# Attention and an ELU network on one core: an order planned in rounds by deadlines, the later pairs' first 64 queries in float16 with DMA transposes, and one copy for the first batches' outputs

## The chip, the core and the metric

The kernel runs on 1 core of a Trainium2 chip. The core's engines run on their own and wait for each other by semaphores: TensorE (PE in the profile; PEld is its loading of stationary operands), VectorE (DVE), ScalarE (ACT), GpSimd (POOL) and SyncE (SP), whose queue issues every DMA of this kernel, one after the other. Times are device microseconds (us) of one execution; lower is better.

## The reference

```python
scores = scale * np.matmul(q, k.transpose(0, 1, 3, 2))        # 8 batches, 8 heads, 576 x 64 each
bias = -(cum[:, :, :, None] - cum[:, :, None, :])             # cum: cumulative sum of max(s, 0)
scores = np.where(causal, -1000000000.0, scores + np.minimum(bias, 0.0))
attn = np.exp(scores - np.max(scores, axis=-1, keepdims=True))
attn = attn / (np.sum(attn, axis=-1, keepdims=True) + 1e-09)
attn_out = np.matmul(attn, v)
x = attn_out.transpose(0, 2, 1, 3).reshape(4608, 512)
h = x @ w_in                                                  # 512 -> 2048
g = np.where(h > 0.0, h, np.exp(np.minimum(h, 0.0)) - 1.0)
out = g @ w_out                                               # 2048 -> 512
```

The two weights come as 64-bit floats, the rest as 32-bit floats.

## The kernel before

**Work.** Attention goes by pairs of heads. A batch's 576 queries are its first 64, of both heads of a pair in one tile of 128 rows (a pair unit, tiles named `_None`), and four blocks of 128 queries per head. The first 320 queries of batches 0 to 2 (12 pairs, the low pairs; tiles `kl`, `sml`, `trl`, `tl`, `avl`, `xl`) are computed in float32. All else, the first 320 queries of batch 3, batches 4 to 7 whole, and the last 256 queries of batches 0 to 3, uses scores and values split in two float16 parts. So 20 pair units (batches 3 to 7) go the later way. For each block PE makes scores (`sc`), DVE adds the mask and finds the row's extreme (`mn`), ACT takes exp, the row is scaled by its inverse sum (`sm`, `sml`), turned, and multiplied by the values (`av`, `avl`); the result goes by `x` or `xl` to `x_dram`.

In a pair unit of before, the probabilities `psh` stay in float32; PE turns them (`tr`, line 1227), ACT or DVE copies the turned tile to `pc` and DVE subtracts to get its rest (`split_pt`, L1157 to L1162), PE multiplies twice (`av_None`, L1220), and `halves` (L1282) takes the wanted quarter-tiles out with two copies and two additions, both of 64x64. A block of 128 queries instead is split in float16 (`halved`) and turned by a DMA (`turned_load`, tile `T`). A low pair's result is put in `xl` by three copies (L890 to L894).

The network runs over 18 chunks of 256 rows. Chunk 0 is in float32 (`h<-x,wa`, `o<-wa,gg`); the others take each product as three float16 products (L1436, L1493), from weights split in two parts (`wp`). Each of the 32 weight units of 512 KB is loaded as raw 64-bit words into one of 4 slots (`raws`), decoded by ACT and DVE (L702, L706, L711), measured (L632, L635), and, when all are there, scaled and split (L437 to L439, L726).

**Order.** Nothing runs in the order of the code. Each operation is recorded with a priority, the engines it may run on and a cost for each (`Plan.op`), and `issue` lays them out: of all operations whose inputs are laid out, it takes the one that could start first by its own costs, of equal ones the one of lower priority number, and fixes the engine and the place. PE's order, for one, is then fixed: a matmul whose input is late holds all behind it. While PE's planned time is under 60 us, gaps are filled with transposes of the identity that nobody reads (`scratch`, L1556).

Of the kernel before, what the change touches and what calls it, by code (L numbers as in the profile page):

```python
# [10 lines left out]
F32R = mybir.dt.float32r  # L11
# [47 lines left out]
class Buf:  # L59


    def __init__(self, pool, shape, dtype, name, tag=None, bufs=1, others=(), always=False):
# [8 lines left out]
        self.users = 0  # L71
        self.until = {}
# [20 lines left out]
class Op:  # L93
    __slots__ = ("ways", "after", "before", "behind", "bufs", "new", "prio", "ready", "left", "filler")


class Plan:
# [45 lines left out]
    def op(self, prio, ways, reads=(), writes=(), late=()):  # L143
# [5 lines left out]
        for accesses, write in ((reads, False), (writes, True)):  # L149
# [10 lines left out]
            for b, part in expanded:  # L160
# [5 lines left out]
                if b not in o.bufs:  # L166
                    o.bufs.add(b)
                    b.users += 1
# [19 lines left out]
        o.left, o.ready = len(o.after) + len(firsts), {}  # L188
# [10 lines left out]

    def issue(self):  # L200
        engines = sorted({self.ENGINE.get(w[0], w[0]) for o in self.ops for w in o.ways})
# [3 lines left out]
        slots, skipped = {}, {}  # L205
        pipe = 0.0
# [13 lines left out]
        while pending:  # L220
# [7 lines left out]
            best = None  # L228
# [5 lines left out]
            for o in pending:  # L234
# [16 lines left out]
                else:  # L251
# [9 lines left out]
                    rank = (start + GAP if o.filler else start, o.prio)  # L261
                    if best is None or rank < best[0]:
                        best = (rank, o, n)
            assert best is not None, "no operation can be issued"
            (start, _), o, n = best
# [8 lines left out]
            if len(o.ways[n]) > 3:  # L274

                pipe = max(pipe, end) + o.ways[n][4] / RATE
                lag = pipe + o.ways[n][3] - end
            self.log.append((engine, start, end, o.prio))
            free[engine] = max(start + 40.0, end - self.OVERLAP.get(engine, 0.0))
            for b, k in o.new:  # L280
                gone = skipped.setdefault(b.home, set())
                gone.add(k)
                while taken[b.home] in gone:
                    gone.remove(taken[b.home])
                    taken[b.home] += 1
                slots.setdefault(b.key, []).append(b)
# [8 lines left out]
            for d in (*o.before, *o.behind):  # L295
                d.left -= 1
                if not d.left:
                    pending.append(d)
            at = len(block.instructions)
# [11 lines left out]
        return max(free.values()), free  # L311
# [53 lines left out]
def kernel(  # L365
# [55 lines left out]
    def rounded(prio, n, dst, src, reads, writes, sign=1.0, only=None):  # L421

        ways = [
            ("Pool", pool_1(n),
             lambda: pool.tensor_scalar(dst(), src(), sign, 1.0, ALU.mult, ALU.mult)),
            ("ACT", act_s(n),
             lambda: act.activation(dst(), src(), AF.Copy, scale=sign)),
            ("DVE-SB", dve_1(n),
             lambda: dve.tensor_scalar(dst(), src(), sign, None, ALU.mult)),
        ]  # L430
        op(prio, [w for w in ways if only is None or w[0] in only], reads, writes)

# [9 lines left out]
    def rest(prio, n, dst, src, hi, reads, writes, only=None):  # L442

        ways = [
            ("DVE-SB", dve_2(n), lambda: dve.tensor_tensor(dst(), src(), hi(), ALU.subtract)),
            ("Pool", pool_2(n), lambda: pool.tensor_tensor(dst(), src(), hi(), ALU.subtract)),
        ]
        op(prio, [w for w in ways if only is None or w[0] in only], reads, writes)
# [166 lines left out]

    def scale_tiles():
# [29 lines left out]
    def scales_of(prio, spans, dst):  # L646
# [20 lines left out]
        op(prio, [("PE", pe4(P), lambda: pe_.matmul(flat.v[:, :P], tops.v, ident, start=True, stop=True))],  # L667
# [174 lines left out]
    def weighing_low(u):  # L842
# [6 lines left out]
        def pair():  # L849
# [3 lines left out]
            op(prio, [("PE", pe4(P), lambda: pe_.matmul(  # L853
                av.v[:HB, n : n + P], u.vs.v[:, 0], turned.v[:, :P], start=True, stop=True))],
               [(turned, "pair"), u.vs], [av])

        def keys(kb):
# [22 lines left out]
            def products():  # L880
                for h in range(2):
                    pe_.matmul(av.v[h * HB : (h + 1) * HB, n - c : n], u.vs.v[:, 1 + 2 * kb + h], dst()[:, h],
# [147 lines left out]
    def prepare(u):  # L1030
# [14 lines left out]
        u.vs = plan.buf(sb, [P, 1, 2, D], F32R, f"vs_{u.tag}", tag="vs0", bufs=NP)  # L1045
        if u.col == 4:
            prio = PRIO_V
        src, used = (lambda: u.va.v[:, j, :1]), values_of(u.va, j)
        rounded(prio, D, lambda: u.vs.v[:, :1, 0], src, used, [u.vs])
        rest(prio, D, lambda: u.vs.v[:, :1, 1], src,  # L1050
             lambda: u.vs.v[:, :1, 0].bitcast(F32), used, [u.vs])
# [105 lines left out]
    def split_pt(prio, tag, tr, w):  # L1157
        pc = plan.buf(sb, [P, 2, w], F32R, f"pc_{tag}", tag="pc")
        psum_copy(prio, w, lambda: pc.v[:, 0], lambda: tr.v[:, :w], [tr], [(pc, 0)])
        op(prio, [("DVE", dve_p(w), lambda: dve.tensor_tensor(  # L1160
            pc.v[:, 1], tr.v[:, :w], pc.v[:, 0].bitcast(F32), ALU.subtract))],
           [tr, (pc, 0)], [(pc, 1)])  # L1162
        return [(pc, 0), (pc, 1)]

    def scoring(u):
# [8 lines left out]
        if u.h is None:  # L1174
            sm = plan.buf(sb, [P, 1], F32, f"sm_{u.tag}", tag="sm", bufs=2)
            psh = u.pp = plan.buf(sb, [P, P], F32, f"psh_{u.tag}", tag="pc")

            def pair():
# [6 lines left out]
                    (sm, 0, True, 1, 1.0), view=lambda v: v.rearrange("p (h t) -> p h t", h=2),  # L1185
# [476 lines left out]
```

## Time and profile before

| | |
|---|---|
| median of 3 runs | 1032.26 us (1030.23 to 1032.54) |
| the profiled execution | 1028.56 us, of which the span of its instructions is 1026.4 us |
| PE busy | 1005.4 us (98%) |
| PEld, DVE, ACT, POOL busy | 67%, 83%, 64%, 24% |

Busy time is the time in which an engine shows at least one instruction. Matmuls overlap each other in their rows, so a wait of PE shows only where it is longer than what is still running.

### The profile page before, as it was taken

The page shows a single profiled execution, that of the slowest core. Times are in us where ns is not written, and L with a number is a line of the kernel's source. Part 1 is how long each engine was busy: PE and PEld are TensorE (multiplying, and loading weights), DVE is VectorE, ACT ScalarE, POOL GpSimd, SP SyncE. Part 2 cuts the span into 40 slices and gives each one's busy share as a digit, 9 for nine tenths or more (in the row PEclk, how much of TensorE's full clock was granted, in tenths as well). Part 3 has the DMA queues.
Part 4 walks back from the last instruction along what each step waited for, and adds up shares of the span by engine and source line. Part 5 has one row for each costly group of instructions (what it writes and reads, how often), then busy time and mean ns, then how long its engine had stood idle before and what let it go on. Part 6 is the DMA issues. An engine that isn't in the chain of part 4 may idle for free. (4 is left out here: it accounts for less than half of the span.)

```text
span 1026.4 us, 21904 instructions
## 1 busy us (share of the span) xinstructions
PE 1005.4 (98%) x7342; PEld 690.3 (67%) x7342; DVE 851.8 (83%) x2394; ACT 661.5 (64%) x1583; POOL 247.0 (24%) x411
## 2 busy tenths in 40 slices
PE   8899999999999999999999999999999999999998
PEld 7666656776666666666666666667666766666665
DVE  6898899888989988889999999898879898763343
ACT  5888746667767777667676777765757666553232
POOL 6231432233232122212422322131212132100000
PEclk9999999999999999999999999999999999999999
DMA  7898324689989998879999999989987998851000
GB/s 204 261 281 258 98 83 129 147 184 238 207 180 190 215 214 186 168 186 230 189 188 207 217 192 192 212 194 202 218 186 178 218 214 177 166 109 48 1 22 21
DMA packets 296725, 179.85 MB, mean 175 GB/s; under 512 B 209908, under 2 KB 270564, under 8 KB 296612
## 3 DMA queue, kind: packets, MB, share of 16 engines
q1 hardware_dynamic: 296612, 178.45, 77.2%
q8 instruction: 58, 0.95, 0.4%
q14 instruction: 55, 0.45, 0.2%
HBM read 93.08 MB, written 36.81 MB: 127 GB/s over the span
## 5 line engine op out<-in xcount | busy, mean ns | idle before, releaser
L1436 PE MATMUL h<-xh,wp 128*128 128x256 f16 x2176 | 398.6, 273 | 0.0
L1493 PE MATMUL o<-wp,gg 128*128 128x512 f16 x1632 | 392.6, 379 | 1.0 <-DVE gg L1475 1.0
L1436 PEld LDWEIGHTS <-wp 128*128 128x128 f16 x3264 | 317.2, 98 | 65.2 <-issue 2.4
L1436 PE MATMUL h<-xl,wp 128*128 128x256 f16 x1088 | 296.5, 273 | 0.7 <-DVE xl L1412 0.7
L1493 PEld LDWEIGHTS <-gg 128*128 128x128 f16 x1632 | 157.9, 98 | 147.1 <-DVE gg L1475 2.9
L1082 ACT ACTIVATE p<-p,mn 128x192 f32<-128x192 f32 (+1 forms) x232 | 143.9, 620 | 65.5 <-DVE mn L1077 59.9
L1142 DVE SCALAR_TENSOR_TENSOR p<-p,sm,p 128x512 f16<-128x512 f32 (+3 forms) x263 | 158.6, 622 | 1.3 <-POOL p L1134 0.3
L1448 ACT ACTIVATE g<-h,cs 128x512 f32<-128x512 f32 x136 | 92.4, 680 | 84.3 <-PE h L1436 83.9
L1472 ACT ACTIVATE gg<-h 128x512 f16<-128x512 f32 x134 | 79.6, 594 | 89.3 <-DVE h L1468 87.8
L1077 DVE CUSTOM_DVE_ANT_0 p<-sc,maskw 128x192 f32<-128x192 f32 (+1 forms) x232 | 109.0, 480 | 11.0 <-PE sc L1074 8.9
L1074 PE MATMUL sc<-set 128*128 128x288 f16 (+3 forms) x544 | 110.8, 298 | 3.3 <-DVE mn L1077 3.2
L1475 DVE SCALAR_TENSOR_TENSOR gg<-h,gg 128x512 f16<-128x512 f32 x136 | 93.2, 686 | 22.8 <-ACT gg L1472 22.1
L1134 POOL TENSOR_SCALAR p<-p,sm 128x64 f16<-128x64 f32 (+3 forms) x77 | 54.2, 707 | 225.9 <-DVE sm L1088 88.8
L1468 DVE SCALAR_TENSOR_TENSOR h<-g,cs,h 128x512 f32<-128x512 f32 x136 | 101.9, 749 | 5.5 <-ACT g L1455 1.4
L1138 ACT ACTIVATE p<-p,sm 128x512 f16<-128x512 f32 (+3 forms) x147 | 78.6, 545 | 18.4 <-ACT p L1082 6.6
L1459 DVE TENSOR_SCALAR g<-g 128x512 f32<-128x512 f32 x98 | 43.2, 441 | 55.2 <-ACT g L1448 54.8
L1074 PEld LDWEIGHTS <-set 128*128 128x128 f16 x584 | 54.7, 98 | 37.8 <-issue 6.0
L1261 PEld LDWEIGHTS <-v 128*64 128x64 f16 x960 | 48.2, 110 | 21.3 <-issue 11.9
L1261 PE MATMUL av<-T,v 128*64 128x256 f16 (+5 forms) x960 | 61.4, 278 | 0.8 <-DMA T<-p 0.8
L437 POOL TENSOR_SCALAR v<-va,scales 128x320 f16<-128x320 f32 (+1 forms) x35 | 24.2, 691 | 115.2 <-PE av L1261 92.7
L437 POOL TENSOR_SCALAR xh<-xc,cs 128x512 f16<-128x512 f32 x23 | 17.3, 753 | 112.8 <-PE h L1436 104.6
L1082 ACT ACTIVATION_READ_ACCUMULATOR p<-p,mn 128x1 f32 x232 | 43.6, 188 | 0.0
(202 smaller groups left out, 1264.0 us busy)
## 6 DMA issues: line engine op xcount, KB each, us to landing
set<-spread SPq DMA_DIRECT2D x32, 432.0 KB
spread<-parts_None SPq DMA_DIRECT2D x32, 288.0 KB
set<-spread SPq DMA_DIRECT2D x32, 288.0 KB
raws<-in_w_in_dram SPq DMA_DIRECT2D x16, 512.0 KB
raws<-in_w_out_dram SPq DMA_DIRECT2D x16, 512.0 KB
out_dram<-ost SPq DMA_DIRECT2D x32, 256.0 KB
va<-in_vb_dram SPq DMA_DIRECT2D x16, 352.0 KB
xc<-x_dram SPq DMA_DIRECT2D x22, 256.0 KB
```

The source lines that it names most:

```text
L1074: pe_.matmul(view(sc.v[:, :cw]), l, r, start=n == 0, stop=n == len(pairs) - 1)
L1077: op(prio, [("DVE", 168 + cw + 55 * (i > 0), lambda i=i, sc=sc: dve.tensor_tensor_reduce(pt.v[:, i * cw : (i + 1) * cw], sc.v[:, :cw], mv( ...
L1082: op(prio, [("ACT", 383 + w / 1.2, lambda: act.activation(pt.v[:, :w], pt.v[:, :w], AF.Exp, bias=mn.v[:, n - 1 : n], scale=-1.0, accum_out ...
L1138: ("ACT", 295 + size / 1.2, lambda part=part: act.activation(part(0), own(part), AF.Copy, scale=sm.v[:, r])),
L1142: ("DVE-SB", dve_2(size), lambda part=part: dve.scalar_tensor_tensor(part(1), own(part), sm.v[:, r], part(0), ALU.mult, ALU.subtract)),
L1261: pe_.matmul(av.v[w.h * HB : (w.h + 1) * HB, dst], w.values.v[:, w.h, kb, v], part(w, kb, m), start=kb == 0 and m == 0 and v == 0, stop=kb ...
L1436: pe_.matmul(columns(k), weight_part(f, 0, part)[1]()[:, c * P : (c + 1) * P], xx.v[:, c], start=(c == 0 and m == 0), stop=(c == NCB - 1 a ...
L1448: op(side, [("ACT", act_c(W) + (0 if native else 90), lambda: act.activation(g.v, hp.v, AF.Exp, scale=1.0 if native else by(3)))], [hp] + ...
L1468: op(side, [("DVE", dve_p(W) + 60, lambda: dve.scalar_tensor_tensor(hp.v, g.v, by(2 if sign[0] else 1), hp.v, ALU.mult, ALU.max))], [g, cs ...
L1472: ("ACT", act_c(W), lambda: act.activation(gg.v[:, 0], hp.v, AF.Copy, scale=2.0**-DOWN)),
L1475: op(side, [("DVE", dve_p(W), lambda: dve.scalar_tensor_tensor(gg.v[:, 1], hp.v, 2.0**-DOWN, gg.v[:, 0], ALU.mult, ALU.subtract))], [hp, ( ...
L1493: pe_.matmul(acc[i].v, gg.v[:, g, at], weight_part(f, 1, part)[1](), start=(f == 0 and m == 0), stop=(f == NF - 1 and m == 2),)
```

## The change

- **Order.** `issue` now lays the operations out up to 12 times without writing anything. After each round `deadlines` goes back through the order from its end: an operation is due (`late`) when the first of those that need its result, or the next in its engine's order on PE, or the one that takes over a buffer that it uses, has to begin. The next round takes, on the engine that could start first, the operation that is due first among those that could start within `WAIT` of it (0 on PE, 30 ns on DVE, ACT and POOL). The first round is the old rule. The round that ends first by the planner's own costs is written.
- **Pair units.** Probabilities are split into two float16 parts (`ph`) by `split_scaled`, turned by one DMA of two units (`th`), and multiplied as three float16 products for each head, 64 columns into 64 rows each (`front_step`), right where the blocks' products (`av<-T`) are made. For batch 3 they share a bank and an eviction with them; for batches 4 to 7 they take a bank (`avh`) and an eviction of 64 columns. The values `vs` are float16 parts too.
- **Low pairs.** The product of the first 64 queries is made in two halves that land where they belong, and one copy of 320 columns replaces three.
- The largest weights' and values' magnitudes are turned by a PE transpose in place of a float32 product with the identity (13 times), and one exp of one column is put at ACT's start (`first_exp`).

```diff
+    def deadlines(self, order, end):
+
+        late = dict.fromkeys(self.ENDS, end)
+        for o in reversed(order):
+            engine, start, stop, lag = o.at
+            t = late.get(engine, end)
+            for d in o.before:
+                if d.at is not None:
+                    t = min(t, d.late - lag - self.HOPS.get((engine, d.at[0]), self.HOP))
+            for b in o.bufs:
+                for d in b.followed:
+                    t = min(t, d.late - lag - self.HOPS.get((engine, d.at[0]), self.HOP))
+            t -= stop - start
...
+    ENDS = ("PE",)
+    ROUNDS, WAIT = 12, {"PE": 0.0, "DVE": 30.0, "ACT": 30.0, "Pool": 30.0, "SP": 0.0}
+
     def issue(self):
+        best = None
+        for n in range(self.ROUNDS):
+            self.reset()
+            self.wait = n > 0
+            end, order = self.run(False)
+            if best is None or end < best[0]:
+                best = end, self.wait, [(o, o.late) for o in self.ops]
+            self.deadlines(order, end)
...
-            (start, _), o, n = best
+                    found.append((start + GAP if o.filler else start, o.prio, self.ENGINE.get(o.ways[n][0], o.ways[n][0]), n, o))
+            first = min(found, key=lambda x: x[:2])
+            until, engine = first[0] + (self.WAIT[first[2]] if self.wait else 0.0), first[2]
+            start, _, _, n, o = min(
+                (x for x in found if x[2] == engine and (x[0] <= until and not x[4].filler or x is first)),
+                key=lambda x: (x[4].late, x[1]))
...
-        op(prio, [("PE", pe4(P), lambda: pe_.matmul(flat.v[:, :P], tops.v, ident, start=True, stop=True))],
+        op(prio, [("PE", 111.0, lambda: pe_.transpose(flat.v[:, :P], tops.v, ident))],
...
-            psum_copy(prio, n, lambda: x.v[:, HB:LOW], lambda: av.v[:, :n], [av], [(x, 2)])
-            for h in range(2):
-                rows, a0 = slice(h * HB, (h + 1) * HB), n + h * HB
-                psum_copy(prio, HB, lambda rows=rows: x.v[rows, :HB],
-                          lambda a0=a0: av.v[:HB, a0 : a0 + HB], [av], [(x, h)])
+            psum_copy(prio, LOW, lambda: x.v[:, :LOW], lambda: av.v[:, :LOW], [av], [x])
...
-                normalize(prio, psh, P, sm, 0)
+                split_scaled(prio, P, lambda m: p16.v[:, m], lambda: psh.v, lambda: sm.v[:, :1],
+                             [sm, (psh, "data")], p16)
+                turned_load(prio, 2, lambda: u.pt.v, lambda: p16.v.rearrange("p m q -> p (m q)"),
+                            [(p16, 0), (p16, 1)], [u.pt])
...
-                for h in range(2):
-                    halves(prio, h, HB, u.x_part((h, 0)), 0, av, h * HB)
...
+                def front_step():
+                    for m, v in ((0, 0), (1, 0), (0, 1)):
+                        for h in range(2):
+                            pe_.matmul(
+                                fav.v[h * HB : (h + 1) * HB, :HB], front.vs.v[:, v], front.pt.v[:, m, h * HB : (h + 1) * HB],
+                                start=m == 0 and v == 0, stop=v == 1,
+                            )
```

How the order moves is seen at three places. The first is SP's queue near the start, where the third low pair's keys wait for their decay sums (`kl<-sums_dram`; of two buffers the number tells the pair: `kl_2` is the third). Before:

```order
L413 DMA kl_3_256<-in_kT_dram 64x2x320
L413 DMA raws<-in_w_in_dram 128x4x256
L413 DMA raws<-in_w_out_dram 128x1024
L413 DMA raws<-in_w_in_dram 128x4x256
L413 DMA raws<-in_w_out_dram 128x1024
L413 DMA kl_2_138<-sums_dram 1x2x320
L413 DMA kl_3_256<-sums_dram 1x2x320
```

The same place of the changed kernel:

```order
L475 DMA kl_3_257<-in_kT_dram 64x2x320
L475 DMA raws<-in_w_in_dram 128x4x256 x2
L475 DMA kl_2_122<-sums_dram 1x2x320
L475 DMA kl_3_257<-sums_dram 1x2x320
L475 DMA raws<-in_w_out_dram 128x1024 x2
```

Two of the four weight units now stand behind the third and fourth pairs' sums. The second place is DVE's order after the second low pair's inverse sums (`sml_1`), towards the third pair's first extreme (`mn_2_0`). Before:

```order
L1088 RECIPROCAL sml_1_314<-sml_1_314 128x5
L453 COPY xl_0_379<-avl_0_319 64x64
L1097 TENSOR_SCALAR pl_1_306<-pl_1_306,sml_1_314 128x128
L1097 TENSOR_SCALAR p_173<-p_173,sml_1_314 128x320
L530 TENSOR_SCALAR aux<-aux 64x576
L706 TENSOR_SCALAR raws<-raws 128x512
L711 SCALAR_TENSOR_TENSOR wa_409<-raws 128x512
```

Two more such decodes follow there before the third pair's first extreme. In the changed kernel, with that extreme as the last row:

```order
L1139 RECIPROCAL sml_1_318<-sml_1_318 128x5
L758 TENSOR_SCALAR raws<-raws 128x512
L1148 TENSOR_SCALAR p_160<-p_160,sml_1_318 128x320
L1148 TENSOR_SCALAR pl_both_1_156<-pl_both_1_156,sml_1_318 128x320
L763 SCALAR_TENSOR_TENSOR wa_413<-raws 128x512
L758 TENSOR_SCALAR raws<-raws 128x512
L684 TENSOR_REDUCE peaks<-wa_413 128x1
L1128 ISA pl_2_430,mn_2_0_431<-sc_2_0_0_421,masks 128x128
```

One decoded weight unit (`wa`) stands ahead of the third pair's first row where three stood. Counted over DVE's whole order, the decoded units ahead of the 1st to 12th low pair's inverse sums were 0, 0, 4, 5, 9, 13, 15, 17, 22, 24, 29, 32 and are 0, 0, 2, 4, 5, 8, 10, 11, 14, 16, 19, 27; the identity transposes in PE's order were 178 and are 155.

The third place is a pair unit on PE. Before, its turning stood in the middle of other work, and the two products some twenty rows later, each alone:

```order
L1493 LDWEIGHTS gg_2_2001
L1493 MATMUL o_1_1927<-wp_1554,gg_2_2001 128x512
L1227 MATMUL tr_0_None_2080<-ident,psh_0_None_2046 128x128
L1074 LDWEIGHTS set_185
L1074 MATMUL sc_0_0_0_1_0_2082<-set_185 128x320
```

In the changed kernel the last of its six float16 products stands ahead of the blocks' first ones (batch 3):

```order
L1298 MATMUL av_0_1_0_2193<-th_0_None_1969,vs_0_None_1526 64x64
L1313 LDWEIGHTS v_0_0_0_1528
L1313 MATMUL av_0_1_0_2193<-T_0_0_0_2055,v_0_0_0_1528 64x256
L1313 LDWEIGHTS v_0_0_0_1528
L1313 MATMUL av_0_1_0_2193<-T_0_1_0_2068,v_0_0_0_1528 64x256
```

The turning is gone from PE, and the products moved to where the blocks' are made. For the 4 pairs of batch 3 they stand against those; for the other 16 some rows of other products lie between.

## Rows read from the trace of the kernel before

**Rows 1.** The page's first part: busy us, share of the span, instructions.

```profile
span 1026.4 us, 21904 instructions
PE 1005.4 (98%) x7342; PEld 690.3 (67%) x7342; DVE 851.8 (83%) x2394; ACT 661.5 (64%) x1583; POOL 247.0 (24%) x411
```

**Rows 2.** The chain that ended last: start us, us, what.

```profile
952.11 2.62 PE h L1436 x24
954.73 2.59 PE o L1493 x12
```

**Rows 3.** Windows: busy us (instructions) of PE, PEld, DVE, ACT, POOL; PEclk; DMA; GB/s.

```profile
0.00:25.00 25.00, 21.93 (x156) 19.64 (x157) 17.15 (x47) 13.45 (x42) 16.50 (x42) 1.00 0.72 204
25.00:50.00 25.00, 22.36 (x148) 15.45 (x147) 20.37 (x69) 20.23 (x62) 5.02 (x14) 1.00 0.87 257
50.00:75.00 25.00, 23.39 (x153) 15.84 (x151) 23.14 (x78) 22.31 (x72) 8.56 (x24) 1.00 1.02 284
75.00:100.00 25.00, 24.34 (x135) 17.59 (x132) 22.61 (x75) 21.79 (x66) 6.24 (x15) 1.00 0.86 259
...
600.00:700.00 100.00, 99.97 (x790) 68.58 (x787) 91.41 (x253) 68.67 (x154) 26.02 (x40) 1.00 0.96 202
```

**Rows 4.** PE's groups by shape: count, busy us, mean ns; idle before, releaser.

```profile
L1436 PE MATMUL h<-xh,wp 128*128 128x256 f16 x2176 | 398.6, 273 | 0.0
...
L1556 PE MATMUL scratch<-ident 128*128 128x128 f32 x177 | 24.2, 292 | 0.0
...
L1227 PE MATMUL tr_None<-ident,psh_None 128*128 128x128 f32 x20 | 5.8, 288 | 1.8 <-POOL psh_None L1095 1.4 <-DVE psh_None L1097 0.2 <-ACT psh_None L1099 0.2
...
L667 PE MATMUL flat<-ident,tops 128*128 128x128 f32 x26 | 5.3, 287 | 0.2 <-ACT tl L452 0.2
```

**Rows 5.** PE's timeline at the start: start us, us, what.

```profile
22.66 4.59 PE L1556 MATMUL scratch<-ident 128*128 128x128 f32 x40
27.08 0.39 PE L1074 MATMUL sc<-kl,low_queries 128*128 128x128 f32 x2
```

**Rows 6.** SP's timeline there: start us, us, what.

```profile
16.57 0.61 SPq L413 DMA_DIRECT2D raws<-in_w_in_dram  x1
...
18.26 0.50 SPq L413 DMA_DIRECT2D raws<-in_w_out_dram  x1
18.87 1.26 SPq L413 DMA_DIRECT2D kl<-sums_dram  x2
```

**Rows 7.** PE's timeline at a pair unit and at a group of blocks' products.

```profile
187.23 0.27 PE L1227 MATMUL tr_None<-ident,psh_None 128*128 128x128 f32 x1
187.34 0.43 PE L1074 MATMUL sc<-set 128*128 128x320 f16 x2
...
191.06 0.83 PE L1261 MATMUL av<-T,v 128*64 128x256 f16 x16
191.82 0.28 PE L1436 MATMUL h<-xh,wp 128*128 128x256 f16 x1
...
193.03 0.27 PE L1436 MATMUL h<-xh,wp 128*128 128x256 f16 x1
193.06 0.42 PE L1220 MATMUL av_None<-pc_None,vs_None 128*128 128x128 f32 x2
193.32 0.28 PE L1436 MATMUL h<-xh,wp 128*128 128x256 f16 x1
```

**Rows 8.** DVE's groups by shape.

```profile
L711 DVE SCALAR_TENSOR_TENSOR wa<-raws 128x512 uint32<-128x512 uint32 x32 | 21.9, 685 | 3.4 <-ACT raws L702 2.7 <-ACT raws L708 0.3
...
L706 DVE TENSOR_SCALAR raws<-raws 128x512 uint32<-128x512 uint32 x31 | 13.4, 436 | 0.0
...
L1289 DVE TENSOR_TENSOR x_None<-av_None,x_None 64x64 f32<-64x64 f32 x40 | 8.7, 219 | 1.9 <-ACT x_None L452 1.4
```

**Rows 9.** The turned tiles; then the page's DMA queue: packets, MB, share.

```profile
L418 SPq DMA_TRANSPOSE T<-p x168: 1203/1318/4976, 177.1 to 913.0; - x168
...
q1 hardware_dynamic: 296612, 178.45, 77.2%
```

**Rows 10.** The split weights: ns min/median/max, first and last start us.

```profile
L1436 PE MATMUL h<-xh,wp x2176: 269/273/284, 145.9 to 1015.0; 128*128 128x256 f16 x198
...
L726 DVE SCALAR_TENSOR_TENSOR wp<-wa,scales,wp x32: 733/740/1627, 125.7 to 164.3; 128x512 f16<-128x512 f32 x32
```

More of the change, by code (lines that the diff above doesn't have):

```diff
@@ L93 @@
 class Op:
-    __slots__ = ("ways", "after", "before", "behind", "bufs", "new", "prio", "ready", "left", "filler")
+    __slots__ = ("ways", "after", "before", "behind", "bufs", "new", "prio", "ready", "left", "filler", "late", "at", "frees")
 class Plan:
@@ L198, in ready, with reset, run @@
         )
-    def issue(self):
+    def reset(self):
+        for o in self.ops:
+            o.ready, o.left = {}, len(o.after)
+            for b in o.bufs:
+                b.users, b.until, b.key, b.bufs = len(b.used_by), {}, b.home, b.home_bufs
+        for o in self.ops:
+            for d in o.behind:
+                d.left += 1
+    def deadlines(self, order, end):
[6 more added lines that the diff above has]
+                    t = min(t, d.late - lag - self.HOPS.get((engine, d.at[0]), self.HOP))
+            for b in o.bufs:
+                for d in b.followed:
+                    t = min(t, d.late - lag - self.HOPS.get((engine, d.at[0]), self.HOP))
+            t -= stop - start
+            for d in o.behind:
+                if d.at is not None:
+                    t = min(t, d.late)
+            o.late = t
+            if engine in late:
+                late[engine] = t
+    ENDS = ("PE",)
+    ROUNDS, WAIT = 12, {"PE": 0.0, "DVE": 30.0, "ACT": 30.0, "Pool": 30.0, "SP": 0.0}
+    def issue(self):
+        best = None
[6 more added lines that the diff above has]
+            self.deadlines(order, end)
+        _, self.wait, lates = best
+        for o, late in lates:
+            o.late = late
+        self.reset()
+        return self.run(True)
+    def run(self, emit):
         engines = sorted({self.ENGINE.get(w[0], w[0]) for o in self.ops for w in o.ways})
@@ L205, in issue @@
         slots, skipped = {}, {}
+        order = []
+        for o in self.ops:
+            o.at = None
+            for b in o.bufs:
+                b.followed = []
         pipe = 0.0
@@ L277, in issue @@
                 lag = pipe + o.ways[n][3] - end
+            o.at = engine, start, end, lag
+            if not o.filler:
+                order.append(o)
             self.log.append((engine, start, end, o.prio))
@@ L310, in issue @@
                 last[i.engine] = i.name
-        return max(free.values()), free
+        return max(free.values()), order
 def pe(n):
@@ L440, in scaled, with split_scaled @@
         ], reads, writes)
[L442 to L448, printed above, removed]
+    def split_scaled(prio, n, dst, src, by, used, parts):
+        scaled(prio, n, lambda: dst(0), src, by, used, [(parts, 0)])
+        op(prio, [("DVE-SB", dve_2(n), lambda: dve.scalar_tensor_tensor(
+            dst(1), src(), by(), dst(0), ALU.mult, ALU.subtract))], [*used, (parts, 0)], [(parts, 1)])
     def psum_copy(prio, n, dst, src, reads, writes, only=None):
@@ L1559 @@
     fillers()
+    first_exp()
     decay_sums()
```

122 lines of the change are left out of this document (50 added, 72 removed).

## The prediction

> **What bounds the kernel now.** I read the page's first part first. PE is busy 98% of the span, DVE 83%, ACT 64% [rows 1]. PE bounds the kernel, and there seem to be 21 us to win. That is too low. In the chain that ended last, 24 products of 256 columns take 2.62 us, so one follows another every 109 ns, and 12 of 512 columns take 2.59 us, 216 ns each [rows 2]; yet a product of 256 columns stands in its row for 273 ns [rows 4]. Rows of PE overlap by 164 ns, and a wait shorter than that shows nowhere.
>
> Then the windows, to see where PE does not do its real work [rows 3]. In the first 100 us it is idle for 25 - 21.93 + 25 - 22.36 + 25 - 23.39 + 25 - 24.34 = 8.0 us, and the identity transposes that nobody reads take another 24.2 us, all in that stretch [rows 4]: 32 us without work. In the same 100 us DVE and ACT rise to 23.1 and 22.3 of 25 us, and the DMA share reaches 1.02. From 600 to 700 us PE is busy 99.97 us, DVE 91.4, DMA 0.96. So there are two stages: a start in which PE waits for DVE, ACT and the loads, and a long rest in which PE has nearly all that it can take, with DVE and DMA close behind. PE's clock is granted at 1.00, its upper level of 2.4 GHz, in all these windows, so no term comes from the clock. Behind 100 us some 21 - 8 = 13 us of visible idle are left, the end of the program among them.
>
> What the change is worth is therefore PE's own work, plus PE's waits, and only so much of DVE's work as PE waits for.
>
> **Pair units on PE.** Before, a turning takes 187.34 - 187.23 = 0.11 us of PE's stream, and the two products lie between two others that start 0.29 us apart, of which 0.11 us belong to the first of them: 0.18 us [rows 7]. That is 0.29 us a unit, 5.8 us for 20. For the new products the nearest row is the group of 16 blocks' products: 0.76 us from 191.06 to 191.82 [rows 7]. They are eight pairs, one for each head, in the two halves of the array: three of 256 columns, three of 192, two of 64, in sum 1472 columns. At 109 ns for 256 columns that is 0.63 us if the two of a pair run side by side, which the 0.76 us bear out; the 0.13 us that are left are the price of entering and leaving that mode. A unit's six products are three pairs of 64 columns, 0.08 us. Four units stand against the blocks' products and pay 0.08; sixteen stand apart and pay 0.21: 0.3 + 3.4 = 3.7 us. Saved: 2.1 us; between 0, if small pairs cost twice as much, and 4.2, if nothing is paid for the mode.
>
> **Other products on PE.** The 13 products with the identity take 26 records [rows 4], two passes each; as transposes one pass of 0.11 us goes: 1.4 us. The low pairs' 12 products of 128 columns, two passes each, become two halves side by side, so 0.11 us less each: 1.3 us, or 0 if the halves don't overlap. Together 2.7, between 1.4 and 2.7.
>
> **The wait at the turning.** PE's order is fixed, and it sat 1.8 us idle before the 20 turnings, for the scaled probabilities [rows 4]; each may hide up to 164 ns more, 5.1 us in all. I take 3. The new products wait for `th`, but they stand behind both heads' scores, next to products that need the heads' own turned tiles, which are made later. So I cost that wait at nothing; the cover is the two heads' softmax. Without it the least is the DMA's issue, 1.3 us [rows 9], once a unit.
>
> **The start.** The order is the largest and least certain term. The third low pair's first score starts at 27.08 us, behind 4.4 us of identity transposes [rows 5]; its decay sums are issued at 18.87 us, right behind four weight units of 512 KB [rows 6]. Now two of the four stand behind it: about 1.1 us less of SP's queue, and 1 MB less ahead of it, which at the 204 to 257 GB/s of these windows [rows 3] is 4 to 5 us. So up to 4.4 us of PE come free here. Further on, six fewer decoded units stand ahead of the 8th pair's sums on DVE; with 436 + 685 ns of DVE for each [rows 8] it has 6.7 us less to do first, where it is busy over 90% [rows 3]. Both in full are 11.1 us. But decodes are moved, not removed: chunk 0 and chunk 1 need them, and what low pairs win early may be paid when the weights are late. Nothing in the profile prices the order as a whole; the bounds are 0 and 11.1, and since the queue's place is a wait that I can point at while the rest is only moved work, I take the middle, 6.
>
> **DVE and ACT.** The 40 additions (8.7 us of DVE [rows 8]), 40 small copies, the copy and the subtraction of each unit go; two subtractions and one small eviction a unit come; a low pair has one copy for three. On DVE some 8 us less of 852 by such rows, and as much on ACT. PE waits for DVE only in what is left of its 13 us, so I take 1 us (0 to 3). The added issues on SP, 20 of 1.3 us, and their traffic lie beside PE's work as long as loads come ahead of need; `first_exp` lies in time in which ACT waits for the first loads. Both: 0.
>
> **Sum.** 2.1 + 2.7 + 3 + 6 + 1 = 14.8 us. The profiled execution took 1028.56 us (its span and 2.2 us around it), so it would take 1013.8; the median of the three runs lies 3.7 us above it, so 1017.5 us. All terms at their low ends give 1028 or so, at their high ends (4.2 + 2.7 + 5.1 + 11.1 + 3 = 26.1) 1006.
>
> **Rivals.**
>
> *The start stays as it is.* The first 100 us are set by how much DVE, ACT and DMA have to do, not by its order; what PE wins at the third pair it loses when chunk 0's weights are decoded. For it: the DMA share of 1.02 and DVE at 92% between 50 and 75 us [rows 3]. Against it: 4.4 us of empty transposes stand right where the queue's order holds a pair back [rows 5, 6]. Then 8.8 us are left: 1023.5.
>
> *More than that.* The new rule also takes half of the 13 us behind 100 us, since it knows which operation PE will need first, and the start gives all 11: 2.1 + 2.7 + 4 + 11 + 7 = 27 us, 1005.5. For it: waits of under 164 ns don't show, so there is more to win than the page says. Against it: DVE and DMA are over 90% busy there, whatever their order.
>
> *Slower: SP's queue and the DMA.* The queue is served in order, and a turning that waits for `ph` holds the loads behind it. Turnings are 168 and become 188; the issue of one takes 1.32 us [rows 9]. If each held back a transfer that PE waits for, the price would be 20 x 1.32 = 26.4 us, and 1017.5 + 26.4 = 1044; it decides from 14.8 / 20 = 0.74 us a turning. The traffic itself is 40 units of 32 KB, 1.3 of 178.45 MB, by bytes 0.6% of the span or 6 us of all 16 engines, and from 600 to 700 us only 4% of them are free [rows 3, 9]. Against it: 168 such turnings pass today, and PE is idle for 0.03 us of that window. Beside this rival stands a rule of the Trainium skill ("VectorE: DVE Perf Modes", Rules for kernel authors): a 128x128 transpose belongs on TensorE where PSUM will do as its destination, since the crossbar DMA takes about 1.3 us against 0.4 us. The trace agrees on the DMA's side (1.32 us), and shows less on PE's, 0.29 us in the row and 0.11 us of the stream [rows 4, 7]; by the rule the turnings should have stayed, which is right only if SP, not PE, is the queue that waits.
>
> *The weights come too late.* The split weights' first low half starts at 125.7 us, and chunk 1's first product at 145.9 us [rows 10]: 20 us of room. With PE some 6 us ahead, 14 are left. The decodes move back by up to ten units (29 to 19 ahead of the 11th pair), 11 us of DVE: not enough. It decides from 14 us on; a slip of 25 would cost 11 us and leave 1028.5.
>
> **Chances.** My forecast 0.48, the start as it is 0.22, more 0.13, slower by SP's queue 0.12, late weights 0.05. A median over a few runs can tell about 0.2%, 2 us, from no change. Faster than that are the first three but for a little of the second (0.02), and a little of the last (0.01): 0.82; the same 0.06; slower 0.12. The range reaches from rival two to the top of what the terms allow, 1004 to 1031, and leaves out the slow case and half of a tenth below. Given the forecast's own case it is 1010 to 1024.
>
> **What would show it.** No row of PE under `tr_None`, and 188 turnings on SP whose waits show on no other engine. The third pair's first score at 23 to 25 us in place of 27.08, with fewer identity transposes before it; busy windows to 100 us with less idle. Chunk 1's first product before 145.9 us, and the low halves of the weights ahead of it. PE's products still 109 and 216 ns apart. I am wrong if chunk 1 starts as late as before (the start's term is nothing), if PE's idle goes to `av<-T` or `sc<-set` behind a DMA, or if the low pairs' halves take as long as the whole.

## The result, and the profile after

The changed kernel takes 1044.15 us, median of 6 runs (1038.37 to 1046.38), beside 1032.4 us of the kernel before (1029.98 to 1034.18): ratio 1.0113, 95% interval 1.0093 to 1.0134. It is slower by 1.1%; the forecast was 1017.5 us. Its profiled execution took 1043.96 us.

The page's first part after the change, to be held against [rows 1]:

```profile
span 1041.9 us, 21915 instructions
...
PE 1000.1 (96%) x7390; PEld 684.7 (66%) x7390; DVE 838.2 (80%) x2327; ACT 652.6 (63%) x1527; POOL 252.6 (24%) x416
```

PE is busy 5 us less in a span that is 15.5 us longer; 3.6 us of the 5 are empty transposes that are left out. So a little work was saved, and PE waits more. Where, the windows say; first those that answer [rows 3], then three long stretches, of after:

```profile
0.00:25.00 25.00, 21.28 (x159) 19.12 (x160) 17.87 (x46) 13.46 (x41) 16.20 (x42) 1.00 0.69 202
25.00:50.00 25.00, 23.20 (x169) 17.13 (x167) 22.48 (x84) 22.36 (x71) 8.18 (x23) 1.00 0.88 251
50.00:75.00 25.00, 24.12 (x166) 19.19 (x165) 23.29 (x78) 23.88 (x75) 10.30 (x28) 1.00 0.99 271
75.00:100.00 25.00, 25.00 (x158) 17.23 (x157) 20.84 (x68) 22.42 (x67) 6.25 (x14) 1.00 0.87 276
...
600.00:700.00 100.00, 98.28 (x762) 66.13 (x760) 88.12 (x239) 67.28 (x146) 20.76 (x34) 1.00 0.96 197
...
0.00:200.00 200.00, 193.19 (x1259) 138.94 (x1260) 179.88 (x522) 150.83 (x409) 81.74 (x159) 1.00 0.70 194
200.00:600.00 400.00, 371.17 (x2807) 249.01 (x2806) 336.14 (x990) 263.48 (x631) 102.78 (x155) 1.00 0.94 194
600.00:1030.00 430.00, 427.91 (x3291) 293.17 (x3289) 318.62 (x811) 235.87 (x484) 68.09 (x103) 1.00 0.68 149
```

and two of the same stretches of before:

```profile
0.00:200.00 200.00, 190.52 (x1159) 134.78 (x1160) 175.75 (x524) 142.30 (x398) 70.70 (x148) 1.00 0.64 182
200.00:600.00 400.00, 393.51 (x2962) 267.27 (x2962) 361.07 (x1069) 282.92 (x692) 106.41 (x155) 1.00 0.94 200
```

PE's groups by shape, and the row of the split weights' high half, of after:

```profile
L1596 PE MATMUL scratch<-ident 128*128 128x128 f32 x154 | 20.6, 289 | 0.0
...
L719 PE MATMUL flat<-ident,tops 128*128 128x128 f32 x13 | 3.7, 281 | 0.6 <-DVE tops L708 0.6
...
L1476 PE MATMUL h<-xh,wp x2176: 269/273/422, 139.2 to 1030.4; 128*128 128x256 f16 x198
```

The third pair's first score in PE's timeline, and the pair units' turnings (ns min/median/max, first and last start us):

```profile
22.54 2.73 PE L1596 MATMUL scratch<-ident 128*128 128x128 f32 x23
25.11 0.39 PE L1125 MATMUL sc<-kl,low_queries 128*128 128x128 f32 x2
```

```profile
L480 SPq DMA_TRANSPOSE th_None<-ph_None x20: 1167/1206/2261, 153.4 to 621.9; - x20
```

The start is won. To 200 us PE is busy 193.19 us, 20.6 of them empty transposes, so 172.6 us of work; before it was 190.52 - 24.2 = 166.3: 6.3 us more. Chunk 1's first product comes at 139.2 us, 6.7 us earlier than in [rows 10]. It is the new rule that does this: in the kernels below that are laid out by it, the same product comes at 137.7 to 144.5 us, and in the two laid out by the old rule at 147.7 and 149.3. The loss is between 200 and 600 us: PE is busy 371.17 us in place of 393.51, 22.3 us less. DVE, ACT and POOL fall with it, and the DMA share is 0.94 both times: no engine took over as the busy one. The waits of that stretch (us in total, times, longest), of after:

```profile
POOL p L1185 <- DMA T<-p: 54.6, 11, 13.2
...
ACT p L1189 <- DMA T<-p: 27.7, 18, 4.2
...
POOL vs_None L487 <- PE avh L1298: 14.6, 4, 11.1
...
POOL vs_None L487 <- PE av L1298: 12.9, 2, 6.9
...
PE sc L1125 <- DVE mn L1128: 11.6, 14, 2.3
...
PE sc L1125 <- DVE mn_None L1128: 2.9, 2, 2.3
...
PE sc_None L1125 <- DVE mn L1128: 1.6, 2, 1.1
```

and of before:

```profile
POOL p L1134 <- DMA T<-p: 26.3, 3, 12.0
...
POOL vs_None L425 <- PE av_None L1220: 9.0, 8, 1.7
...
PE sc L1074 <- DVE mn L1077: 2.2, 3, 1.2
...
ACT p L1138 <- DMA T<-p: 1.6, 2, 1.1
```

PE's scores wait 11.6 + 2.9 + 1.6 = 16.1 us for DVE's `mn`, where they waited 2.2: 14 of the 22.3 us. Behind that, two things come later than they did: the buffer of split probabilities `p`, which is free when the DMA has turned what it held, and the buffers of the pair units' values `vs`, which are free when PE has used them. How the first comes to PE is seen in one place, in the timelines of SP, ACT, DVE and PE of after; that the other waits came about in the same way is not shown:

```profile
380.08 4.95 SPq L480 DMA_TRANSPOSE T<-p  x3
...
387.18 0.61 ACT L1189 ACTIVATE p<-p,sm 128x384 f16<-128x384 f32 x1 [2.30 <-DMA T<-p]
...
387.20 0.35 DVE L1187 TENSOR_SCALAR p<-p,sm 128x256 f16<-128x256 f32 x1 [2.48 <-DMA T<-p]
...
389.39 0.35 DVE L1128 CUSTOM_DVE_ANT_0 p<-sc,maskw 128x192 f32<-128x192 f32 x1
...
387.35 0.27 PE L1476 MATMUL h<-xh,wp 128*128 128x256 f16 x1
...
389.80 0.54 PE L1125 MATMUL sc<-set 128*128 128x448 f16 x2 [2.18 <-DVE mn L1128]
```

Three turnings hold SP for 4.95 us. ACT and DVE, whose order is fixed, stand 2.30 and 2.48 us before a tile that is still being turned. DVE, with five other operations to do first, starts its next `mn` at 389.39 us, and PE, whose order is fixed too, stands 2.18 us before a score that waits for it, with the network's products behind it.

### The profile page after: what moved, and what is told of

Same layout as the page of the kernel before. It is cut to its first block, busy times and chain, and to the rows that moved or that the text cites. A ratio compares the mean times of both kernels' runs of the same rounds, so it can differ in the third digit from the quotient of the medians.

```text
span 1041.9 us, 21915 instructions
## 1 busy us (share of the span) xinstructions
PE 1000.1 (96%) x7390; PEld 684.7 (66%) x7390; DVE 838.2 (80%) x2327; ACT 652.6 (63%) x1527; POOL 252.6 (24%) x416
## 5 line engine op out<-in xcount | busy, mean ns | idle before, releaser
L1193 DVE SCALAR_TENSOR_TENSOR p<-p,sm,p 128x512 f16<-128x512 f32 (+3 forms) x255 | 150.5, 617 | 18.5 <-ACT p L1189 10.0
L1515 DVE SCALAR_TENSOR_TENSOR gg<-h,gg 128x512 f16<-128x512 f32 x136 | 93.3, 686 | 26.9 <-ACT gg L1512 26.4
L1185 POOL TENSOR_SCALAR p<-p,sm 128x512 f16<-128x512 f32 (+3 forms) x77 | 52.7, 687 | 251.1 <-DMA T<-p 55.8
L1189 ACT ACTIVATE p<-p,sm 128x64 f16<-128x64 f32 (+3 forms) x153 | 81.0, 539 | 43.2 <-DMA T<-p 28.1
L1499 DVE TENSOR_SCALAR g<-g 128x512 f32<-128x512 f32 x81 | 35.2, 435 | 58.9 <-ACT g L1488 58.4
L1313 PEld LDWEIGHTS <-v 128*64 128x64 f16 x960 | 52.7, 110 | 22.0 <-issue 16.1
```

The source lines that it names most:

```text
L1189: ("ACT", 295 + size / 1.2, lambda part=part: act.activation(part(0), own(part), AF.Copy, scale=sm.v[:, r])),
L1193: ("DVE-SB", dve_2(size), lambda part=part: dve.scalar_tensor_tensor(part(1), own(part), sm.v[:, r], part(0), ALU.mult, ALU.subtract)),
L1313: pe_.matmul(av.v[w.h * HB : (w.h + 1) * HB, dst], w.values.v[:, w.h, kb, v], part(w, kb, m), start=kb == 0 and m == 0 and v == 0, stop=kb ...
L1515: op(side, [("DVE", dve_p(W), lambda: dve.scalar_tensor_tensor(gg.v[:, 1], hp.v, 2.0**-DOWN, gg.v[:, 0], ALU.mult, ALU.subtract))], [hp, ( ...
```

## The experiments

All ratios are to the kernel before, run on the same chip.

**Is it the order?** Three kernels: the old rule with all new operations; the new rule with all old operations; the new rule told a higher price of the DMA.

```diff
-    ROUNDS, WAIT = 12, ...
+    ROUNDS, WAIT = 1, ...
```

> The changed kernel with one planning round, so the order is laid out by the old rule; all its new operations stay. Theory A (the deadline order puts the attention stage further ahead than the DMA engines can feed it between 200 and 600 us, and 20 more turnings add some 8 to 11 us of DMA time there): the order's gain at the start (11 us) and most of its loss behind it (31 us) go, PE's own work stays 6 us shorter, so 1024 to 1034 us. Rival B (the 20 added turnings alone cause the loss, by SP's queue or by their traffic): the loss stays and the start's gain goes, 1048 to 1058 us. Rival C (the order alone, whatever the DMA): 1022 to 1028 us, 6 us under the kernel before.

1048.53 us, 1.0147 (1.0106 to 1.0187).

The second is the kernel before with the change's `deadlines`, `reset`, `run` and `issue` and nothing else.

> The kernel before with all its own operations (pair units turned by PE, three copies for a low pair), laid out by the new rule of 12 rounds. Theory A: the start's gain of 11 us comes, the loss behind it comes too, smaller by the traffic of 20 turnings: 1034 to 1044 us. Rival B (the turnings alone): the start's gain without the loss, 1018 to 1024 us. Rival C (the order alone): 1046 to 1054 us.

1029.48 us, 0.9966 (0.9948 to 0.9985).

```diff
-LAG, RATE = 4000.0, 285.0
+LAG, RATE = 4000.0, 255.0
-                   units * P * P * 2.2)], reads, writes)
+                   units * P * P * 3.15)], reads, writes)
```

> The changed kernel, with two of its planner's numbers nearer to what the trace shows of the DMA: 255 in place of 285 bytes per ns, and 3.15 in place of 2.2 as a turning's factor (202 in place of 126 ns a unit). Nothing but the order changes. Theory A: the planner sees that the DMA engines are short and puts network products where PE now waits for turned tiles, 1020 to 1034 us. Rival B: the same turnings, so 1042 to 1046 us. Rival C: by its prices an order is still made by deadlines, 1038 to 1048 us.

1042.18 us, 1.0093 (1.0065 to 1.012). Theories A and C fall: the rule gains 2.5 to 4.4 us with either set of operations, each read from one order, prices mend nothing, and the new operations cost 15 to 17 us under either rule. Rival B has the first and the third; the second missed its 1018 to 1024 us.

**What of a turning counts?** Three kernels in the changed kernel's order replace all 188 turnings by plain copies. The first has long pieces:

```diff
-lambda: nc.sync.dma_start_transpose(dst(), src())
+lambda: nc.sync.dma_start(dst(), src())
```

> The changed kernel in its own order, with every DMA that turns replaced by a plain copy of as many bytes to the same tile in long pieces. The turning is left out, so the probabilities are not turned; the work of all engines is otherwise the same. Theory A: the DMA engines have some 35 us less to do between 200 and 600 us and PE's waits there fall from 46 us towards 15: 1012 to 1026 us. Rival B: the same, 1012 to 1026 us. Rival C (the order alone, whatever the DMA): 1040 to 1046 us.

1005.81 us, 0.9742 (0.9714 to 0.9771). The second keeps small pieces of 256 bytes (but for 40 of the copies), the third adds two copies of 16 bytes to each long one:

```diff
+        for n in range(2):
+            nc.sync.dma_start(tiny[at[0] : at[0] + 1], ident[:1, :4])
+            at[0] += 1
         return nc.sync.dma_start(dst, src)
```

> The changed kernel in its own order, every DMA that turns replaced by a plain copy, this time in pieces of 256 bytes to the places where the turning writes them (but for 40 of 188, which stay in one piece); the turning is left out. It has nearly as many packets as the turnings, and a shorter issue on SP. Theory D by way of the DMA engines' packets: 1030 to 1044 us. Theory D by way of SP's queue, where the issue of a turning takes 1.32 us and that of a copy 0.5: 1004 to 1012 us. Rivals E and F say the same as the copies in long pieces gave, 1005.8 us, only if neither packets nor issues matter.

> The changed kernel in its own order, every DMA that turns replaced by a plain copy in long pieces, with two copies of 16 bytes issued ahead of each, so that SP's queue is held about as long for each turning as before (some 1.4 us) and the DMA engines have nothing more to do; the turning is left out. Theory D by way of SP's queue: 1030 to 1046 us. Theory D by way of the DMA engines' packets: 1005 to 1012 us.

1007.24 us, 0.9754 (0.9722 to 0.9787), and 1038.2 us, 1.0051 (1.0031 to 1.0071). The stretch from 200 to 600 us in the first, the second and the third:

```profile
200.00:600.00 400.00, 398.88 (x3090) 268.47 (x3089) 372.42 (x1082) 287.08 (x686) 112.17 (x164) 1.00 0.75 212
```

```profile
200.00:600.00 400.00, 399.06 (x3093) 269.01 (x3091) 370.71 (x1082) 287.38 (x686) 110.74 (x164) 1.00 0.91 212
```

```profile
200.00:600.00 400.00, 378.00 (x2876) 251.47 (x2874) 344.20 (x1006) 267.43 (x640) 107.83 (x159) 0.99 0.69 198
```

PE is busy 399 us with a DMA share of 0.91, and 378 with 0.69. So how busy the DMA engines are is not what PE waits for; holding SP's queue is enough to bring back 32 of the 38 us that the plain copies had won. Nor is it how long a copy is under way: by the semaphores in the traces the second kernel's copies land 4.1 us after their issue began, in the median of this stretch, the third's 2.3 us, and the turnings of the changed kernel 3.8. (The third kernel adds issues, the time of issues, and waits: SP waits there 36 us in all for earlier copies to land, 5 us or less in the other two. Which of these counts was not parted.)

**Which of the new operations?** The pair units of before, with all else of the change:

```diff
-                turned_load(prio, 2, lambda: u.pt.v, ...)
+                normalize(prio, psh, P, sm, 0)
...
+                op(prio, [("PE", 111.0, lambda: pe_.transpose(tr.v[:, :P], u.pp.v, ident))], ...)
+                pieces = split_pt(prio, u.tag, tr, P)
```

> The changed kernel with the pair units of before (turned by PE, four small evictions), and all else of the change: the new rule, the low pairs' one copy, the transposes of magnitudes, the early exp. Theory D (the new rule is worth some 3 us, the 20 turnings by DMA cost what was lost, as the stage's turnings pass a queue and DMA engines that are nearly full): 1023 to 1029 us. Rival E (the new pair units lose it by other means than the DMA: their buffers, and products that stand behind both heads): the same here. Rival F (the low pairs' new products and copy, or the early exp, lose it): 1038 to 1046 us.

1022.8 us, 0.9907 (0.9874 to 0.994). So what loses time is in the pair units; theories D and E said the same of this run and are still to be parted. Without the new rule, too:

```diff
-    ROUNDS, WAIT = 12, ...
+    ROUNDS, WAIT = 1, ...
```

> Old pair units and the old rule, with the change's small edits alone: low pairs' halves and one copy, transposes of magnitudes, early exp. The kernel with these and the new rule took 1022.8 us, the one with the new rule alone 1029.5. If rule and small edits add up, the small edits are worth 6.7 us: 1025 to 1027 us. If they only count together (the new rule uses the room that the one copy makes): 1029 to 1033 us.

1029.28 us, 0.9973 (0.9953 to 0.9992): rule and small edits are worth some 3 us each by themselves and 11 together, so they count together more than they add up to. Theory F falls.

**The turning on PE, with the new products.**

```diff
+                    for m in range(2):
+                        pe_.matmul(tr.v[:, m * P : (m + 1) * P], u.p16.v[:, m], ident16, start=True, stop=True)
...
+                psum_copy(prio, 2 * P, lambda: u.pt.v.rearrange("p m q -> p (m q)"), lambda: tr.v[:, : 2 * P], [tr], [u.pt])
```

> The changed kernel with its new pair units, whose two float16 parts are turned on PE (two products with an identity of 128 columns into one bank, one eviction of 256 columns) in place of the DMA; nothing else differs. Theory D: 20 turnings fewer on SP's queue, some 2 us more on PE and 8 us more on ACT or DVE: 1022 to 1030 us. Rival E: 1038 to 1046 us. Rival F: 1038 to 1046 us.

1039.12 us, 1.0061 (1.0032 to 1.009): theory D's figure is missed by 9 us. How much of that is one order's accident, the same reshuffle shows for this kernel, the changed one and the one with old pair units:

```diff
-"DVE": 30.0, "ACT": 30.0, "Pool": 30.0
+"DVE": 45.0, "ACT": 45.0, "Pool": 45.0
```

> The kernel with new pair units turned on PE, laid out again with 45 in place of 30 ns of the rule's leeway, which only reshuffles the order. In its first order it was as fast as the kernel with old pair units up to the tenth chunk (684 us) and lost 15 us behind it. If that loss is an accident of one order (theory D): another order gives 1020 to 1032 us. If the new pair units lose it by their buffers and places (rival E): 1036 to 1044 us again.

> The changed kernel itself, laid out again with 45 in place of 30 ns of leeway. Theory D: the loss between 200 and 600 us is one of turnings on a full queue, which no reshuffle takes away: 1038 to 1050 us. If the loss is an accident of one order: anywhere from 1018 to 1045 us, most likely under 1036.

> Old pair units with all else of the change, laid out again with 45 in place of 30 ns of leeway. If its 1022.8 us are the kernel's and not one order's: 1018 to 1028 us, within the 5 to 8 us by which two orders of the other kernels differed. If an accident: 1029 to 1036 us.

1034.44 us, 1.0016 (1.0001 to 1.0032); 1051.76 us, 1.0189 (1.0151 to 1.0226); 1018.35 us, 0.9869 (0.9829 to 0.991). The first lies between what D and E said of it, the second 2 us above D's range, the third in its range. Two orders of one kernel differ by 4.4 to 7.6 us. What lies between the kernels is larger in the mean of both orders: 1020.6 us with the old pair units, 1036.8 with the new ones turned on PE, 1048.0 with the new ones turned by DMA. Both theories D and E hold a part of it.

**Another queue for the 20 turnings.**

```diff
-                turned_load(prio, 2, ...)
+                op(prio, [("ACT", 1330.0, lambda: act.dma_start_transpose(u.pt.v, ...), ...)], ...)
```

> The changed kernel with the 20 pair turnings issued by ACT's own DMA queue in place of SP's; they stay DMA transposes with the same packets. Theory D, by way of SP's queue (its issues fill some 91% of the stretch from 200 to 600 us, and turnings are over half of them): SP gets 26 us back, ACT, which has room, gives 26: 1024 to 1034 us. By way of the DMA engines' own turning work, wherever it is issued: 1040 to 1046 us. Rival E (the new pair units' buffers and places in the order, not their turning): 1038 to 1046 us.

1084.46 us, 1.0522 (1.0503 to 1.054), which nobody expected. SP's waits from 200 to 700 us there:

```profile
SPq L480 <- DMA th_None<-ph_None: 75.0, 15, 7.3
```

and its stretch from 200 to 600 us:

```profile
200.00:600.00 400.00, 356.71 (x2639) 239.33 (x2637) 320.54 (x914) 238.34 (x563) 100.00 (x143) 0.96 0.81 178
```

SP's turnings wait, by semaphore, until the one that ACT issued has landed, 5 us in the mean, and all loads behind them with it. PE, idle more often, also gets less clock: 0.96 in the mean of the stretch, where the changed kernel has 1.00, so a part of the loss may be the clock's.

**The values and the place of the products.** The first two kernels give the values 8 buffers (their room comes from one low tile that moves to another tag; with the turning by DMA `ph` has two as well); the other two make the products at once, in a step of the pair unit's own:

```diff
-tag="vs0", bufs=NP)
+tag="vs0", bufs=2 * NP)
```

> The changed kernel with 8 in place of 4 buffers for the pair units' values and 2 in place of 1 for their split probabilities. Theory H (the new products stand behind both heads' turned tiles, so the values are held longer, and POOL, whose work is in order, waits 39.5 us for them, after 18.1 before): POOL's wait for them goes and the time falls by 6 to 14 us to 1030 to 1038 us. Theory D alone (turnings on SP's queue and the DMA): 1040 to 1050 us.

> New pair units turned on PE, with 8 in place of 4 buffers for their values. Theory H: 1022 to 1030 us, as with the old pair units. If the rest of the new units costs it: 1033 to 1040 us, as in the two orders without the buffers.

```diff
+        if u.h is None:
+            def early():
+                fav = plan.buf(ps, [P, 512], F32, f"avh_{u.tag}", tag="av", bufs=N_AV)
...
-        front = u.front if not first else None
+        front = None
```

> The changed kernel with the pair units' new products made as soon as their own turned tile is there, into a bank of the av kind, with an eviction of their own, as before made its two products; batch 3's, too, get one of their own. Theory H (the place behind both heads): 1028 to 1038 us. Theory D alone: 1040 to 1050 us.

> As the last, with the turning on PE: the new pair units differ from the old only in that two float16 parts are made ahead of the turning and three half-width products follow. Theory H: 1018 to 1028 us. If what the new units make DVE, ACT and POOL do costs it: 1033 to 1040 us.

With buffers 1039.38 us, 1.0067 (1.005 to 1.0083), and 1026.97, 0.9952 (0.9937 to 0.9967); with early products 1043.85 us, 1.0114 (1.008 to 1.0147), and 1032.47, 1.0 (0.9987 to 1.0013). Beside both orders of the like kernel, more buffers are worth 5 to 12 us with either turning; the early place 0.3 to 8 us with the DMA and 2 to 7 on PE, which is about what two orders of one kernel differ by. Theory H's range is met once in four, by more buffers on PE; with the DMA it is missed by 1.4 us (and theory D's by 0.6), and both early kernels miss it, by 6 and 4 us, the one with the DMA being where theory D alone had it. Its way is met only in part: with more buffers POOL waits for PE's products no more, but in the stretch from 200 to 600 us it now waits for `scales`, on which the new values depend; with the DMA, then on PE:

```profile
POOL p L1185 <- DMA T<-p: 32.6, 11, 8.3
...
POOL vs_None L487 <- DVE scales L724: 17.7, 2, 13.7
```

```profile
POOL vs_None L487 <- DVE scales L726: 13.9, 3, 9.2
...
POOL p L1187 <- DMA T<-p: 3.1, 3, 1.3
```

**The price of a turning by itself.** To the kernel with old pair units, 20 turnings that nobody reads:

```diff
+        if not u.blocks[0] and u.h == 0 and i == u.last:
+            turned_load(prio, 2, lambda: extra.v, lambda: t16.v[:, col : col + 2 * P], used, [extra])
```

> Old pair units with all else of the change, and 20 further turnings of two units, one for each pair of batches 3 to 7, into a tile that nobody reads. Theory D (a turning costs by what it takes of SP's queue and the DMA's order, some 0.6 us each): 1030 to 1038 us. If a turning costs only through those who wait for its result: 1020 to 1027 us.

1030.92 us, 0.9988 (0.9961 to 1.0014): 8.1 us over 1022.8 and 12.6 over 1018.35, so 0.4 to 0.6 us a turning, though nobody waits for its result. It is a rough figure: what two orders differ by, 4.4 to 7.6 us, is 0.2 to 0.4 us a turning, and each of them also holds the buffer of `p` that it reads.

## Why the prediction was wrong

**The failed step.** "The added issues on SP, 20 of 1.3 us, and their traffic lie beside PE's work as long as loads come ahead of need ... Both: 0." The issues were costed right (1.206 us in the median after) and their cover was assumed. Their queue was nearly full already: summed over SP's single issues from 200 to 600 us, with whatever an issue waits within its own row, they took 343 of 400 us before, 175 of them turnings, and 365 after. Little cover was left. (The sum alone does not tell the loss: with the copies of 16 bytes it is 320 us, and PE loses as much, but there SP also stands 36 us before copies that have not landed.) The like kernels differ by

| new pair units | by DMA | on PE | difference |
|---|---|---|---|
| first order | 1044.15 | 1039.12 | 5.0 |
| second order | 1051.76 | 1034.44 | 17.3 |
| 8 buffers for the values | 1039.38 | 1026.97 | 12.4 |
| products at once | 1043.85 | 1032.47 | 11.4 |

11.5 us in the mean; the 20 unread turnings cost 8 to 13. The Trainium skill ("VectorE: DVE Perf Modes", Rules for kernel authors) would have kept these transposes on TensorE; the runs bear its advice out for this kernel.

How far the network is by 600 us parts the two turnings better than the time of one order does. The products with the split weights `wp` that PE has made by then (of 4896; the number behind the x), first in the changed kernel, then in its second order, with the turning on PE, with the old pair units, and with those and 20 unread turnings:

```profile
0.00:600.00 600.00, 366.43 (x2343) 1.00 0.86 194
```

```profile
0.00:600.00 600.00, 369.92 (x2366) 1.00 0.85 194
```

```profile
0.00:600.00 600.00, 384.97 (x2462) 1.00 0.84 197
```

```profile
0.00:600.00 600.00, 387.52 (x2466) 0.99 0.85 198
```

```profile
0.00:600.00 600.00, 385.32 (x2441) 0.99 0.84 195
```

All six kernels whose pair units are turned by SP's DMAs have 2334 to 2380, and all nine that turn them on PE, old or new and without unread turnings, 2425 to 2483. PE's busy time to 600 us, less the empty transposes, parts them in the same way: 544 to 551 us against 558 to 563. So to 600 us the loss comes with the DMA's turning, and the new products by themselves cost nothing that shows. The unread turnings take only 25 to 42 of the hundred products that are missing: the rest goes with turnings for whose tiles somebody waits, and in which way was not parted.

**A second step.** "So I cost that wait at nothing; the cover is the two heads' softmax." PE hardly waits at the new products, but what they hold was not costed: the values stay until both heads are turned, with 4 buffers for them. Twice the buffers give back 4.8 and 12.4 us with the DMA (from either order), 12.2 and 7.5 on PE, 9 in the mean. How that reaches PE is not shown: with the turning on PE the network is as far by 600 us as with the old pair units, and what is lost is lost behind that. The 4 to 9 us from there to the old pair units are not explained; they are about what two orders differ by.

**The slow rival.** It gave 1044, which is the time measured, but that it met it to the microsecond is luck: its 26.4 us stood for turnings alone, at the full length of an issue, and on top of all gains. Turnings cost some 0.6 us each (0.4 to 0.6 unread, and 11.5 us for 20 beside the turning on PE), under its own 0.74; 20 unread ones bring the kernel with old pair units back to the time of before (0.9988), not past it. Its argument against itself, that PE is idle for 0.03 us between 600 and 700 us, read the wrong stretch: the pair units' turnings run from 153 to 622 us.

**The start** came as said: 6.3 us more work done by 200 us, for 6. The third pair's first score is at 25.11 us, against [rows 5], and 154 empty transposes are left of 177. The rival with the start as it is falls, and so does the one with late weights. Of the signs of being wrong one came in part: PE's idle went to `sc<-set`, though behind DVE's `mn` and not straight behind a DMA.

**PE's own work** fell: no `tr_None` is left, and the 13 products with the identity have one record each, as said. A low pair's halves take 0.26 us of PE's stream (18.63 to 18.89 us) where the whole took 0.36 (18.21 to 18.57), so 0.10 less for a forecast 0.11. The new pair products saved less than the 2.1 us of the sum. One of the sixteen that stand apart, of after:

```profile
361.61 0.27 PE L1476 MATMUL h<-xh,wp 128*128 128x256 f16 x1
361.81 0.28 PE L1298 MATMUL avh<-th_None,vs_None 128*64 128x64 f16 x6
362.03 0.28 PE L1476 MATMUL h<-xh,wp 128*128 128x256 f16 x1
```

Its neighbours start 0.42 us apart, of which 0.11 belong to the first: 0.31 us, where the prediction had 0.21. Those of batch 3 take 0.12 (171.50 to 171.62 us) for 0.08. Together that is 5.4 us beside 5.8 before, so 0.4 saved. The prediction's low end is off too: its terms at their lowest are 1.4 to 3.2 us, which gives 1029 to 1031, not 1028. The rest of the change, without the pair units, is worth 11 to 15 us (1022.8 and 1018.35, beside 1033.4 of the kernel before on the same chips); for those parts the sum had 2.7 + 6 and a part of DVE's 1. The kernel with the old pair units is the fastest one found that still turns its tiles, faster than before and after. Its page and its stretch from 200 to 600 us, in the second order:

```profile
span 1016.3 us, 21838 instructions
...
PE 996.2 (98%) x7332; PEld 686.3 (68%) x7332; DVE 843.1 (83%) x2355; ACT 664.1 (65%) x1584; POOL 268.8 (26%) x440
...
200.00:600.00 400.00, 394.40 (x2976) 268.20 (x2974) 362.90 (x1072) 285.91 (x704) 118.77 (x175) 1.00 0.96 203
```

## What to carry to other kernels

A queue that issues DMAs is an engine: sum its issues and its waits over the stretch in question before anything is added to it, since the page doesn't count them as busy. When a product is moved behind others, cost what its operands hold meanwhile, not only what it waits for. And where a planner lays out the order, run a second order of the same kernel before a difference of a few us is put down to an edit.

## What the runs showed of the hardware

The size of a DMA's pieces hardly mattered here, and what held SP's queue did: with plain copies in small pieces the kernel took 1007.24 us at a DMA share of 0.91 between 200 and 600 us, in long ones 1005.81 at 0.75, and in long ones with two tiny copies each 1038.2 at 0.69. Turnings from two queues did not overlap in this program: SP's waited 75.0 us in all, at semaphores, for ACT's to land; what the chip would do without that wait no run here shows. The Trainium skill ("DMA: Bandwidth & Descriptors", Silent corruption: two transposing streams in flight at once) says that the later stream must wait for the earlier one to complete; the waits in the trace agree with that. They made a second queue for turnings a loss here, 1084.46 us.
